# Cluster attention and expert layers on one core: a third of the exponential units take an fp16 upper part written by ScalarE, and leave out the product of the two low parts

## The chip, the core and the metric

The kernel runs on one core of one Trainium2 chip. The metric is device time in microseconds (us) of one launch. The engines are named as in the profile: PE (TensorE matmuls), PEld (its weight loads), DVE (VectorE), ACT (ScalarE), POOL (GpSimd) and SP (the DMA queue that most loads are issued on).

## The reference, cut to what matters

Attention over 4 batches, 8 heads, 768 positions, 64 numbers a head, with a mask that lets a query see only keys of its own cluster. Its output goes through a two-level mixture of 16 experts, one expert a row.

```
q_assign = argmax(q_n . c_n); k_assign = argmax(k_n . c_n)
mask   = q_assign[:, :, :, None] == k_assign[:, :, None, :]
scores = where(mask, q @ k.T / sqrt(64), -1e9)
attn   = exp(scores - max(scores)); attn /= sum(attn) + 1e-9
out    = attn @ v
x      = out as 3072 rows of 512
y      = combined gate * (relu(x @ w1[e]) @ w2[e])      # e: the row's expert
```

## The kernel before, in words

**Two stages.** The attention stage takes 32 (batch, head) pairs one after the other; the text calls them heads 0 to 31. Then an expert stage streams the 16 experts' weights from HBM. Everything in fp32 is carried as an upper part and a low part in 16 bits each, so that matmuls run on 16-bit operands.

**A head is 9 units.** The 768 x 768 scores of a head are cut into 9 units of 128 keys x 512 queries. For each unit u of head h the program records `fine(h, u)`, one or two units of `coarse` of a later head, `av` of the unit five before (`LAG = 5`), and then what is due `beside`: loads, splitting of q, k and v into parts, cluster assignment, masks, router logits.

- `fine`: PE makes the scores of the unit into a PSUM tile `psf` (two buffers; L346 and L347). ACT takes the exponential into an SBUF tile `p32` in fp32 (L351; the profile calls it `p`). The upper part `ph` is no tile of its own: it is every second 16-bit word of `p32`, read as bf16. POOL (for five units of each of the last two heads DVE) subtracts it from `p32` and writes the low part `pl` in fp16 (L353).
- `coarse`: PE makes scores of a later head into `psc` (two buffers; L304) and DVE takes row maxima of them (L307).
- `av`: for each of the unit's four blocks of 128 queries, four matmuls of 64 or 65 columns add to the head's output `pso`: `ph` and `pl`, each against the upper part of v (`vh`, 65 columns, one of them of ones for the denominator) and against its low part (`vl`, 64 columns). Each has a weight load of its own.

**What sets the order.** The program text gives each instruction a priority; a scheduler then places the instructions on the engines, each engine in order. So an instruction more on one engine can move others, on that engine and on the rest. `p32`, `pl` come from a pool of seven buffers each.

Of the kernel before, what the change touches and what calls it, by code (L numbers as in the profile page):

```python
# [11 lines left out]
F16 = mybir.dt.float16  # L12
BF16 = mybir.dt.bfloat16
# [9 lines left out]
P = 128  # L23
# [9 lines left out]
def attention(ctx, tc, qT, kT, vr, cen, R, DEN, cfg):  # L33
    nc = tc.nc
# [4 lines left out]
    NCH = S // P  # L39
# [10 lines left out]
    EARLY = ()  # L50
    GAP, RM, RL = 1, 2, 8
    DVE_LO = [()] * 8
    DVE_END = (0, 2, 4, 6, 8)

    const = ctx.enter_context(tc.tile_pool(name="aconst", bufs=1))
# [3 lines left out]
    pp = ctx.enter_context(tc.tile_pool(name="pp", bufs=LAG + 2))  # L59
# [275 lines left out]
    def fsegs(u):  # L335

        return [(r % NCH, r // NCH * (S // 2) + x0, r // NCH * (S // 2) + x1) for r, x0, x1 in segs(u, S // 2)]

    def fine(h, u):
        assert ("max", h) in ready  # L340
        pf = ps_f.tile([P, 512], F32, name="psf")
        off = 0
        for (c, q0, q1) in fsegs(u):
            o = pf[:, off:off + q1 - q0]
            ks = slice(c * P, (c + 1) * P)
            nc.tensor.matmul(out=o, lhsT=KA[h % 8][0:82, ks], rhs=QA[h % 8][0:82, q0:q1], start=True, stop=False)  # L346
            nc.tensor.matmul(out=o, lhsT=KBs[h][:, ks], rhs=QBs[h][:, q0:q1], start=False, stop=True)  # L347
            off += q1 - q0
        p32 = pp.tile([P, 512], F32, name="p32")
        pl = pp.tile([P, 512], F16, name="pl")  # L350
        cfg["exp"] = nc.scalar.activation(out=p32, in_=pf, func=AF.Exp, scale=QK / (SQ * SQ))  # L351
        ph = p32.bitcast(BF16)[:, 1::2]
        lo = (nc.vector if u in (EARLY if h < 2 else DVE_LO[h % 8] if h < NH - 2 else DVE_END) else nc.gpsimd).tensor_tensor(out=pl, in0=p32, in1=ph, op=ALU.subtract)  # L353
        if lo.ins.engine == ET.Pool:
            cfg["lo"] = lo
        Ph[h, u], Pl[h, u] = ph, pl

    def av(h, u):

        vt = V[(h // 2) % 4]  # L360
        off = 0
        ph, pl = Ph.pop((h, u)), Pl.pop((h, u))
        if u == 0:
            Os[h] = ps_o.tile([P, 512], F32, name="pso")
        O = Os[h]
        for (c, q0, q1) in fsegs(u):
            vh, vl = vt[:, h % 2, c, 64:129], vt[:, h % 2, c, 0:64]
            for q in range(q0 // P, q1 // P):
                bs = slice(off, off + P)
                col = q * OW  # L370
                for i, p in enumerate((ph, pl)):
                    nc.tensor.matmul(out=O[:, col:col + 65], lhsT=p[:, bs], rhs=vh, start=c == 0 and q == 0 and i == 0, stop=False, skip_group_check=True)  # L372
                    nc.tensor.matmul(out=O[:, col:col + 64], lhsT=p[:, bs], rhs=vl, start=False, stop=c == NCH - 1 and i == 1, skip_group_check=True)  # L373
                off += P
        if u == 8:
            finish(h)

    def finish(h):

        O = Os.pop(h)  # L380
        b, hh = h // H, h % H
        if hh == 0:
            XSt[b] = xsp.tile([P, NCH, 2, H * D], F16, name="xs")
        Ov = O[:, 0:NCH * OW].rearrange("p (c w) -> p c w", w=OW)
        den = DEN[:, h]
        nc.vector.tensor_scalar(out=den, in0=Ov[:, :, 64], scalar1=EPS, scalar2=1.0 / XS, op0=ALU.add, op1=ALU.mult)
        rec = sm.tile([P, NCH], F32, name="rec")
        nc.vector.reciprocal(out=rec, in_=den)
        xs = XSt[b][:, :, :, hh * D:(hh + 1) * D]
        x = Ov[:, :, 0:64]  # L390
        nc.vector.tensor_tensor(out=x, in0=x, in1=rec.broadcast_to([P, NCH, D]), op=ALU.mult)
        nc.scalar.copy(out=xs[:, :, 0], in_=x)
        nc.vector.tensor_tensor(out=xs[:, :, 1], in0=x, in1=xs[:, :, 0], op=ALU.subtract)
# [94 lines left out]
    def av_next(g):  # L488
        h, u = prev.pop(0)
        av(h, u)  # L490
        if u == 8:
            b, hh = h // H, h % H
            last = b == B - 1 and hh == H - 1
            if last:
                cfg["xs"] = XSt[b]
            if hh == H - 1:
                R.store(b, XSt[b])
            if hh % 2 == 1:
                gens = [R.logits(b, XSt[b], hh // 2, [(ps_m, "psm"), (ps_f, "psf")] if last else None)]
                if hh == H - 1 and not last:  # L500
                    XSt.pop(b)
                    gens += [R.decide(b, then=(lambda: go(now[0], cfg["first"]())) if b == B - 2 else None)]
                at(g + RL, go, g + RL, itertools.chain(*gens))
# [5 lines left out]
    for h in range(NH):  # L509
        for u in range(9):  # L510
            fine(h, u)
            while n < min(9 * NH, g + 1 + min(AHEAD, AHEAD0 + g // 4)):
                coarse(n // 9, n % 9)
                if n % 9 == 8:
                    at(g + 1, go, g + 1, rowmax(n // 9))
                n += 1
            prev.append((h, u))
            if len(prev) > LAG:
                av_next(g)
            beside(g)  # L520
            g += 1
# [846 lines left out]
def tile_cluster_attention_moe(ctx, tc, qT, kT, vr, cen, wr, w1, w2, out):  # L1368
# [25 lines left out]
    with ExitStack() as c:  # L1394
        attention(c, tc, qT, kT, vr, cen, R, DEN, cfg)
# [53 lines left out]
```

## Time and profile before

| | |
|---|---|
| time, median of 3 runs | 765.72 us (764.88 to 766.91) |
| the profiled execution: its own time | 770.1 us |
| its span, first to last instruction | 768.3 us |
| mean granted TensorE clock | 0.984 |
| busy over the span: PE / PEld / DVE / ACT / POOL | 95% / 82% / 79% / 61% / 65% |
| attention stage, first to last L346 matmul | 24.9 to 418 us |

The profiled execution is 1.8 us longer than its span, and 4.4 us longer than the median of the runs. Busy shares are means over both stages; "idle before" in the rows below is the time that an engine stood still just before the instructions of a group, with what ended most of it. A busy PE is not PE at its peak, because matmuls are pipelined: one record lasts some 190 ns while the next begins 30 ns later.

### The profile page before, as it was taken

Reading aid. Unit: us, or ns where it says so; the run is one execution under the profiler, and the core shown is the slowest. Engines: PE = TensorE matmul, PEld = TensorE weight load, DVE = VectorE, ACT = ScalarE, POOL = GpSimd, SP = SyncE. Lnnn points to the kernel's source line nnn. Section 1 sums busy time; section 2 is a strip of 40 time slices with the busy share of each in tenths; the row PEclk is TensorE's granted clock in tenths of the full one; section 3 lists DMA queues with packets and bytes.
Section 4 is the critical chain, followed back from the end, with each engine's and each line's share of the span. In section 5 each row is a group of like instructions: output and inputs, shape, how many; then the busy total and the mean of one; then the engine's idle time right before and its main releaser. Section 6 shows DMA issues by size and latency. Waiting matters only on the chain. (4 is left out here: it accounts for less than half of the span.)

```text
span 768.3 us, 26718 instructions
## 1 busy us (share of the span) xinstructions
PE 731.0 (95%) x11086; PEld 626.9 (82%) x11086; DVE 605.7 (79%) x1209; ACT 466.6 (61%) x910; POOL 499.6 (65%) x522
## 2 busy tenths in 40 slices
PE   5899999999999999998999989999999999999996
PEld 3667888878888788886778777788779999999996
DVE  5887978899788997988866645867588898889861
ACT  4556876868778687674977346435534455555542
POOL 9577778779887798876884425526555556655532
PEclk9889999999999999999999999999999999999999
DMA  8857424545345461231420489866777788888821
GB/s 247 198 144 182 127 74 125 157 112 142 72 129 171 92 147 52 65 126 61 112 80 3 99 270 311 262 212 211 242 236 237 239 272 262 263 277 277 260 81 49
DMA packets 80392, 128.28 MB, mean 167 GB/s; under 512 B 8851, under 2 KB 47251, under 8 KB 80264
## 3 DMA queue, kind: packets, MB, share of 16 engines
q1 hardware_dynamic: 74492, 113.12, 50.7%
q0 software_dynamic: 5616, 13.35, 5.0%
q8 instruction: 88, 1.44, 0.9%
q14 instruction: 40, 0.33, 0.2%
q10 hardware_dynamic: 156, 0.03, 0.0%
HBM read 93.20 MB, written 14.11 MB: 140 GB/s over the span
## 5 line engine op out<-in xcount | busy, mean ns | idle before, releaser
L353 POOL TENSOR_TENSOR pl<-p 128x512 f16<-128x512 f32 x278 | 286.3, 1048 | 86.0 <-ACT p L351 81.1
L307 DVE TENSOR_REDUCE mpart<-psc 128x1 f32<-128x512 f32 (+1 forms) x282 | 190.2, 683 | 34.9 <-PE psc L304 34.8
L351 ACT ACTIVATE p<-psf 128x512 f32<-128x512 f32 x288 | 168.8, 595 | 58.2 <-PE psf L347 54.1
L372 PE MATMUL pso<-V,p 128*128 128x65 f16 x1152 | 162.6, 194 | 0.0
L372 PE MATMUL pso<-V,pl 128*128 128x65 f16 x1152 | 162.1, 194 | 0.0
L373 PE MATMUL pso<-V,pl 128*128 128x64 f16 x1152 | 161.9, 192 | 0.0
L373 PE MATMUL pso<-V,p 128*128 128x64 f16 x1152 | 161.8, 192 | 0.0
L346 PE MATMUL psf<-A 82*128 82x384 f16 (+2 forms) x576 | 145.7, 278 | 4.8 <-ACT p L351 3.2
L347 PE MATMUL psf<-B 128*128 128x384 f16 (+2 forms) x576 | 146.3, 278 | 0.0
L373 PEld LDWEIGHTS <-p 128*128 128x128 bf16 x1152 | 113.1, 98 | 21.7 <-issue 0.7
L372 PEld LDWEIGHTS <-p 128*128 128x128 bf16 x1152 | 112.6, 98 | 8.8 <-issue 0.8
L373 PEld LDWEIGHTS <-pl 128*128 128x128 f16 x1152 | 113.2, 98 | 0.4
L304 PE MATMUL psc<-A 80*128 80x512 f16 (+1 forms) x376 | 109.6, 332 | 4.1 <-DVE mpart L307 2.9
L372 PEld LDWEIGHTS <-pl 128*128 128x128 f16 x1152 | 111.7, 97 | 0.3
L959 DVE SCALAR_TENSOR_TENSOR hl<-psh,hh 128x160 f16<-128x160 f32 (+14 forms) x136 | 50.1, 371 | 60.3 <-ACT hh L958 60.1
L958 ACT ACTIVATE hh<-psh 128x160 f16<-128x160 f32 (+14 forms) x136 | 46.5, 347 | 69.0 <-PE psh L956 68.6
L956 PE MATMUL psh<-xT,wh0a 128*128 128x288 f16 (+7 forms) x512 | 74.7, 255 | 0.0
L347 PEld LDWEIGHTS <-B 128*128 128x128 f16 x576 | 57.4, 100 | 14.7 <-issue 6.4
L956 PE MATMUL psh<-xT,wh0b 128*128 128x272 f16 (+6 forms) x448 | 65.2, 254 | 0.9 <-ACT xT L930 0.9
L346 PEld LDWEIGHTS <-A 82*128 82x128 f16 x576 | 56.3, 99 | 11.0 <-issue 1.1
L918 POOL DMA_INDIRECT xg<-xbuf,ri x32 | 40.8, 1274 | 36.2 <-issue 17.8
L956 PE MATMUL psh<-xT,wl0a 128*128 128x288 f16 (+7 forms) x256 | 64.0, 255 | 0.0
(311 smaller groups left out, 1752.5 us busy)
## 6 DMA issues: line engine op xcount, KB each, us to landing
st<-w SPq DMA_DIRECT2D x128, 512.0 KB
B<-parts SPq DMA_DIRECT2D x64, 192.0 KB
kx<-kT SPq DMA_DIRECT2D x16, 384.0 KB
qx<-qT SPq DMA_DIRECT2D x16, 384.0 KB
vx<-vr SPq DMA_DIRECT2D x16, 384.0 KB
A<-parts SPq DMA_DIRECT2D x32, 192.0 KB
xbuf<-xs SPq DMA_DIRECT2D x4, 1536.0 KB
A<-mk SPq DMA_DIRECT2D x56, 24.0 KB
```

What stands on the lines that cost most here:

```text
L304: last["mm"] = nc.tensor.matmul(out=pc[:, off:off + k1 - k0], lhsT=QA[h % 8][0:80, c * P:(c + 1) * P], rhs=KA[h % 8][0:80, k0:k1], start=T ...
L307: nc.vector.tensor_reduce(out=(mp[:, 0, 0:1], mp[:, :, 1], mp[:, 1, 0:1])[i], in_=pc.rearrange("p (a x) -> p a x", a=n), axis=AX.X, op=ALU ...
L346: nc.tensor.matmul(out=o, lhsT=KA[h % 8][0:82, ks], rhs=QA[h % 8][0:82, q0:q1], start=True, stop=False)
L347: nc.tensor.matmul(out=o, lhsT=KBs[h][:, ks], rhs=QBs[h][:, q0:q1], start=False, stop=True)
L351: cfg["exp"] = nc.scalar.activation(out=p32, in_=pf, func=AF.Exp, scale=QK / (SQ * SQ))
L353: lo = (nc.vector if u in (EARLY if h < 2 else DVE_LO[h % 8] if h < NH - 2 else DVE_END) else nc.gpsimd).tensor_tensor(out=pl, in0=p32, in ...
L372: nc.tensor.matmul(out=O[:, col:col + 65], lhsT=p[:, bs], rhs=vh, start=c == 0 and q == 0 and i == 0, stop=False, skip_group_check=True)
L373: nc.tensor.matmul(out=O[:, col:col + 64], lhsT=p[:, bs], rhs=vl, start=False, stop=c == NCH - 1 and i == 1, skip_group_check=True)
L918: self.got = nc.gpsimd.indirect_dma_start(out=xg[0:n].rearrange("p a d -> p (a d)"), out_offset=None, in_offset=bass.IndirectOffsetOnAxis( ...
L956: self.mm = nc.tensor.matmul(out=ph[:, 0:M], lhsT=w[:, k, fs], rhs=xT[:, a, k], start=i == 0, stop=i == 3 * KD - 1)
L958: nc.scalar.activation(out=hh[:, f], in_=ph[:, 0:M], func=AF.Relu)
L959: self.ev = nc.vector.scalar_tensor_tensor(out=hl[:, f], in0=ph[:, 0:M], scalar=0.0, in1=hh[:, f], op0=ALU.max, op1=ALU.subtract)
```

## The change

For units 1, 4 and 7 of every head (`WHOLE16`) ACT writes the upper part as an fp16 tile `ph` of its own, with a copy from `p32` that rounds; POOL (or DVE) subtracts that tile. In `av` of these units the fourth product, `pl` against `vl`, is not made: three matmuls for each block of queries instead of four. The other six units of a head stay as they are. The new tile has three buffers.

```diff
+    WHOLE16 = 1, 4, 7
...
         cfg["exp"] = nc.scalar.activation(out=p32, in_=pf, func=AF.Exp, scale=QK / (SQ * SQ))
-        ph = p32.bitcast(BF16)[:, 1::2]
+        if u in WHOLE16:
+            ph = pp.tile([P, 512], F16, name="ph", bufs=len(WHOLE16))
+            nc.scalar.copy(out=ph, in_=p32)
+        else:
+            ph = p32.bitcast(BF16)[:, 1::2]
         lo = (nc.vector if u in (EARLY if h < 2 else DVE_LO[h % 8] if h < NH - 2 else DVE_END) else nc.gpsimd).tensor_tensor(out=pl, in0=p32, in1=ph, op=ALU.subtract)
...
-                for i, p in enumerate((ph, pl)):
-                    nc.tensor.matmul(out=O[:, col:col + 65], lhsT=p[:, bs], rhs=vh, start=c == 0 and q == 0 and i == 0, stop=False, skip_group_check=True)
-                    nc.tensor.matmul(out=O[:, col:col + 64], lhsT=p[:, bs], rhs=vl, start=False, stop=c == NCH - 1 and i == 1, skip_group_check=True)
+                prods = [(ph, vh), (ph, vl), (pl, vh)] + ([] if u in WHOLE16 else [(pl, vl)])
+                for i, (p, v) in enumerate(prods):
+                    nc.tensor.matmul(out=O[:, col:col + v.shape[-1]], lhsT=p[:, bs], rhs=v, start=c == 0 and q == 0 and i == 0, stop=c == NCH - 1 and i == len(prods) - 1, skip_group_check=True)
```

Five lines more stand above these places, so L351 becomes L352, L353 becomes L358 and L372/L373 become L378; the new copy is L355.

The order on PE, in `av` of unit 1 of head 0, the first unit that the change touches. Before, a block of 128 queries is eight rows (`p_566` is the unit's `p32`):

```order
L372 LDWEIGHTS p_566
L372 MATMUL pso<-V_173,p_566 128x65
L373 LDWEIGHTS p_566
L373 MATMUL pso<-V_173,p_566 128x64
L372 LDWEIGHTS pl
L372 MATMUL pso<-V_173,pl 128x65
L373 LDWEIGHTS pl
L373 MATMUL pso<-V_173,pl 128x64
```

In the changed kernel a block of the same unit is six rows:

```order
L378 LDWEIGHTS ph
L378 MATMUL pso<-V_173,ph 128x65
L378 LDWEIGHTS ph
L378 MATMUL pso<-V_173,ph 128x64
L378 LDWEIGHTS pl
L378 MATMUL pso<-V_173,pl 128x65
```

The last weight load and the last matmul of 64 columns are gone, here and in 383 other blocks; PE has 384 loads and 384 matmuls less.

The order on ACT, from the exponential of unit 4 of head 8 to the one of unit 7 and what follows it. Before (L351 is the exponential, L200 a half of a split, L222 and L180 splits of v, q and k, L392 the upper part of a head's output, L599 a copy for the router):

```order
L351 ACTIVATE p_3309<-psf 128x512
L222 ACTIVATE V_176<-vx 128x12x64
L351 ACTIVATE p_3357<-psf 128x512
L200 ACTIVATE psm<-vx 128x384
L351 ACTIVATE p_3389<-psf 128x512
L392 CAST xs<-pso 128x6x64
L351 ACTIVATE p_3421<-psf 128x512
L180 ACTIVATE parts<-qx 128x768
L180 ACTIVATE parts<-kx 128x768
```

The changed kernel at the same place, from the exponential of unit 4 on (L355 is the new copy, L201 the half split, L223 and L181 the splits):

```order
L352 ACTIVATE p_3263<-psf 128x512
L201 ACTIVATE psm<-vx 128x384
L355 CAST ph<-p_3263 128x512
L352 ACTIVATE p_3313<-psf 128x512
L223 ACTIVATE V_176<-vx 128x12x64
L352 ACTIVATE p_3345<-psf 128x512
L397 CAST xs<-pso 128x6x64
L352 ACTIVATE p_3373<-psf 128x512
L201 ACTIVATE psm<-vx 128x384
L355 CAST ph<-p_3373 128x512
L352 ACTIVATE p_3407<-psf 128x512
L181 ACTIVATE parts<-qx 128x768
```

Two copies have come in, each with a half split between its exponential and itself; the split of v and the two splits of q and k stand an exponential later than before. Over the whole kernel ACT has 96 copies more; 53 stand right behind their exponential, 43 have another instruction between.

## Rows read from the trace of the kernel before

**Rows 1.** The page: busy time of each engine over the whole span, and the granted TensorE clock in 40 slices, in tenths of full speed.

```profile
PE 731.0 (95%) x11086; PEld 626.9 (82%) x11086; DVE 605.7 (79%) x1209; ACT 466.6 (61%) x910; POOL 499.6 (65%) x522
...
PEclk9889999999999999999999999999999999999999
```

**Rows 2.** Busy time of each engine in the attention stage, 24.9 to 418.2 us: stretch, its length, then busy us (and instructions) of PE, PEld, DVE, ACT and POOL, the granted clock, the DMA share and GB/s.

```profile
24.90:418.20 393.30, 377.38 (x7135) 313.58 (x7134) 336.85 (x733) 292.01 (x561) 306.27 (x298) 0.98 0.42 113
```

**Rows 3.** What PE waited for from 20 to 423 us: us in total, times, the longest.

```profile
PE psm L655 <- DVE roe L643: 4.1, 3, 1.4
PE psf L346 <- ACT p L351: 3.2, 5, 1.6
PE psc L304 <- DVE mpart L307: 2.9, 6, 0.8
```

**Rows 4.** The timeline of PE in head 14: start, us of the record, line. The rows left out are 14 more `av` matmuls of the same unit.

```profile
212.94 0.19 PE L372 MATMUL pso<-V,p 128*128 128x65 f16 x1
...
213.39 0.19 PE L373 MATMUL pso<-V,pl 128*128 128x64 f16 x1
213.42 0.33 PE L346 MATMUL psf<-A 82*128 82x384 f16 x1
```

**Rows 5.** Groups of instructions of the whole kernel: line, engine, operation, shapes, how many | busy us, mean ns of one | idle time before them. The weight loads of both parts, and the subtraction on POOL.

```profile
L353 POOL TENSOR_TENSOR pl<-p 128x512 f16<-128x512 f32 x278 | 286.3, 1048 | 86.0 <-ACT p L351 81.1
...
L373 PEld LDWEIGHTS <-p 128*128 128x128 bf16 x1152 | 113.1, 98 | 21.7 <-issue 0.7
...
L373 PEld LDWEIGHTS <-pl 128*128 128x128 f16 x1152 | 113.2, 98 | 0.4
```

**Rows 6.** Groups of ACT from 20 to 423 us, each shape apart, in the same columns: the exponential, a split that reads SBUF and writes 768 columns of fp16, and a scaling that reads 512 columns of SBUF.

```profile
L351 ACT ACTIVATE p<-psf 128x512 f32<-128x512 f32 x288 | 168.8, 595 | 58.2 <-PE psf L347 54.1 <-POOL pl L353 2.9 <-PE psc L304 0.5
...
L180 ACT ACTIVATE parts<-qx 128x768 f16<-128x768 f32 x14 | 11.8, 840 | 3.7 <-PE psm L241 2.8 <-DMA vx<-vr 0.8
...
L787 ACT ACTIVATE psm<-st 128x512 f32<-128x512 f32 x16 | 9.7, 605 | 0.0
```

**Rows 7.** A timeline of DVE and ACT in head 14: an ACT instruction that waits for a DVE result.

```profile
203.20 0.17 DVE L313 TENSOR_REDUCE m<-mpart 128x6 f32<-128x18 f32 x1
...
203.41 0.21 ACT L317 ACTIVATE mh<-m 128x6 f16<-128x6 f32 x1 [0.25 <-DVE m L313]
```

**Rows 8.** The timeline of ACT where head 8 ends and head 9 begins (at 140.2 us): start, us, line, in brackets the idle time before.

```profile
139.49 0.84 ACT L180 ACTIVATE parts<-qx 128x768 f16<-128x768 f32 x1 [0.32 <-DMA vx<-vr]
140.24 0.83 ACT L180 ACTIVATE parts<-kx 128x768 f16<-128x768 f32 x1
140.97 0.58 ACT L351 ACTIVATE p<-psf 128x512 f32<-128x512 f32 x1
141.45 0.49 ACT L200 ACTIVATE psm<-vx 128x384 f32<-128x384 f32 x1
141.86 0.59 ACT L351 ACTIVATE p<-psf 128x512 f32<-128x512 f32 x1
142.34 0.80 ACT L599 COPY xTr<-psm 128x768 f16<-128x768 f16 x1
143.11 0.99 ACT L266 ACTIVATE mk<-psm,mbias,mscale 128x768 f16<-128x768 f16 x1
144.00 0.20 ACT L317 ACTIVATE mh<-m 128x6 f16<-128x6 f32 x1
144.10 1.24 ACT L351 ACTIVATE p<-psf 128x512 f32<-128x512 f32 x2
```

**Rows 9.** Busy time of the engines head by head, in the columns of rows 2. A stretch begins with the first L346 matmul of its head, to a tenth of a us. First heads 11 to 18, then heads 28 to 31.

```profile
166.20:177.90 11.70, 11.51 (x236) 9.62 (x233) 10.67 (x22) 8.14 (x17) 10.90 (x11) 1.00 0.49 121
177.90:189.50 11.60, 11.50 (x234) 9.56 (x231) 11.56 (x27) 9.89 (x21) 11.12 (x12) 1.00 0.67 189
189.50:202.80 13.30, 13.26 (x258) 11.25 (x255) 10.05 (x23) 10.88 (x20) 11.50 (x13) 1.00 0.29 62
202.80:213.40 10.60, 10.60 (x207) 8.83 (x204) 9.17 (x20) 8.25 (x18) 9.57 (x10) 1.00 0.44 119
213.40:224.70 11.30, 11.30 (x234) 9.53 (x231) 9.07 (x18) 7.49 (x16) 9.37 (x10) 1.00 0.27 70
224.70:236.40 11.70, 11.60 (x237) 9.67 (x234) 11.66 (x27) 10.08 (x21) 9.47 (x10) 1.00 0.69 188
236.40:249.40 13.00, 12.97 (x255) 11.10 (x252) 9.67 (x22) 10.27 (x19) 9.33 (x10) 1.00 0.49 167
249.40:262.00 12.60, 11.24 (x219) 9.25 (x216) 12.39 (x35) 8.02 (x18) 8.45 (x9) 1.00 0.23 67
...
372.50:383.50 11.00, 11.00 (x215) 9.23 (x212) 9.47 (x21) 9.62 (x19) 10.63 (x11) 1.00 0.33 58
383.50:397.40 13.90, 12.10 (x221) 10.08 (x218) 9.34 (x24) 10.29 (x20) 13.32 (x14) 0.95 0.35 92
397.40:409.00 11.60, 10.80 (x215) 9.20 (x213) 8.49 (x18) 10.51 (x21) 6.23 (x8) 0.91 0.08 24
409.00:418.20 9.20, 9.20 (x187) 8.26 (x187) 6.46 (x15) 8.08 (x15) 4.15 (x4) 1.00 0.02 4
```

**Rows 10.** Who waited from 20 to 423 us, in the columns of rows 3: ACT for the scores.

```profile
ACT p L351 <- PE psf L347: 54.1, 94, 2.3
```

**Rows 11.** A group of POOL from 20 to 423 us: the one other subtraction of an fp16 tile from an fp32 one.

```profile
L187 POOL TENSOR_TENSOR V<-vx,V 128x768 f16<-128x768 f32 x1 | 1.6, 1587 | 0.0
```

## The prediction

> **What bounds the kernel now.** I read the page's busy shares first. Over the whole span PE is busy 95%, ACT 61% [rows 1]; the change touches the attention stage alone, so I took that stage by itself: of 393.30 us PE is busy 377.38, DVE 336.85, POOL 306.27, ACT 292.01 [rows 2]. Then the list of what PE waits for. It is short: 4.1 us for a DVE result of the router, 3.2 us for exponentials, 2.9 us for row maxima [rows 3]. Then whether a busy PE there is a full one, since its records overlap: in the timeline the sixteen `av` matmuls of a unit begin from 212.94 to 213.39, 0.45 us for 15 steps, and the scores of the next unit begin 0.03 us after the last [rows 4]. PE has no gap there. In heads 14 and 15 it is busy 10.60 of 10.60 and 11.30 of 11.30 us [rows 9]. So PE sets the pace of this stage, and a matmul that is not made is time saved, as long as no other engine takes over.
>
> That other engine is looked for head by head, because a mean over the stage hides it. DVE is full in heads 12 and 16 (11.56 of 11.60, 11.66 of 11.70) and nearly in head 18 (12.39 of 12.60); ACT has its most in heads 12, 13, 16 and 17 (9.89 of 11.60, 10.88 of 13.30, 10.08 of 11.70, 10.27 of 13.00) and again in 28, 30 and 31 [rows 9]. Yet ACT mostly waits for PE: exponentials waited 54.1 us for scores [rows 10].
>
> **What the rule on occupancy would make of it.** In head 15, where PE is busy 11.30 of 11.30 us, the weight loads are busy 9.53 us, 84%; over the stage 313.58 of 393.30, 80% [rows 2, 9]. The Trainium skill (Perfetto Trace Analysis, Identifying the Most-Contended Engine) says that matmul occupancy is a bad measure of how near TensorE is to its limit, and that the share of weight loads should be read instead. By that rule PE would have a fifth of the stage spare and the saving would come out of slack, for no change at all; by the timeline PE has no gap at 84%. Here the steps of 30 ns decide, and the rule goes into a rival below.
>
> **What the change removes.** 3 units x 32 heads x 4 blocks = 384 matmuls of 64 columns with their loads. One step is 0.45 / 15 = 0.030 us [rows 4]: 384 x 0.030 = **11.5 us**, or 0.36 us a head. The remaining loads read contiguous fp16 in place of every second 16-bit word; loads of the strided `p` and of the contiguous `pl` take 98 ns each [rows 5], so the step should stay.
>
> **What it adds on ACT.** 96 copies, 128x512 from fp32 to fp16. The trace has none of this form. From above: a split of 768 columns takes 840 ns; from below and near it: a scaling of 512 columns from SBUF takes 605 ns, an exponential of 512 columns 595 ns [rows 6]. I take 0.60. What a copy costs ACT depends on its place. Independent ACT instructions overlap by 0.10 us (the exponential at 140.97 lasts 0.58 and the next begins at 141.45 [rows 8]). A copy right behind its exponential can't overlap it: it waits for its end and some 0.04 us for the signal (a DVE result at 203.20 + 0.17 is taken up by ACT at 203.41 [rows 7]; this case has no ACT instruction that waits for the one before it). So 53 copies put 0.64 us between the exponential and what follows, and 43 with another instruction between put 0.50: 33.9 + 21.5 = 55.4 us, 0.58 a copy, 1.73 us a head. At nothing it can't be costed everywhere, and in full it can't cost either: 393.30 - 292.01 = 101 us of ACT are free [rows 2], but not where they are needed.
>
> **Where ACT falls short.** For each head of rows 9 I set the length less 0.36 (what PE would now need) against ACT's busy time plus 1.73. Short are head 12 (11.24 against 11.62: 0.38), head 16 (11.34 against 11.81: 0.47), head 28 (10.64 against 11.35: 0.71), head 30 (11.24 against 12.24: 1.00) and head 31 (8.84 against 9.81: 0.97). Heads 13, 14 and 17 have only 0.33, 0.26 and 0.64 to spare; heads 11, 15, 18 over 1.4. The same pattern of splits, masks and router work comes every 8 heads, so I count rows 11 to 18 three times for heads 3 to 26: 3 x 0.85 + 2.68 = 5.2 us. That is the lower end of what ACT takes back, for it lets ACT work at 100% of a head.
>
> The upper end goes by the one head in which PE waited for exponentials and ACT was the fuller engine: head 30, ACT 10.51 of 11.60 us, 0.906 [rows 9]. If ACT can never be filled beyond that, a head lasts (ACT + 1.73) / 0.906 where this is more: 1.59 over in head 12, 0.98 in 13, 0.78 in 14, 1.70 in 16, 0.61 in 17, 1.89 in 28, 2.27 in 30, 1.99 in 31. 3 x 5.66 + 6.15 = 23.1 us.
>
> I take a value nearer the lower end: 5.2, and 0.35 more in each of the nine heads like 13, 14 and 17, 3.2 us, together **8.4 us**. Two rows speak for the lower end. ACT ran without a gap from 139.49 to 145.34 [rows 8] and in head 13, the same place of the pattern, PE is busy 13.26 of 13.30 us [rows 9]: the two `psf` buffers carry PE over a late exponential of about a unit. And ACT's busy time counts a lone instruction in full, where in a queue 0.10 of it overlaps. What speaks for more is that two copies enter just this stretch, 1.1 us of delay against buffers that hold about one unit.
>
> **What is late next, and the rest.** The delayed exponential is waited for by PE (the scores after next want its `psf`), and through it by DVE. In heads 10, 18 and 26 DVE leaves 0.21 us of the 0.36 (12.39 of 12.60 [rows 9]): 3 x 0.15 = 0.45 us lost. In 12 and 16 DVE leaves 0.04, but there ACT's shortage has taken the saving already, so it isn't counted twice. The subtraction now waits for the copy, up to 0.64 us later; behind it on POOL stand the subtractions of the next units, and `av` five units on waits for them. POOL stood idle 86.0 us before its subtractions, nearly all of it for exponentials [rows 5], and PE's list holds no wait for `pl` [rows 3], so this costs nothing; without that cover it would be up to 96 x 0.64 = 61 us. The subtraction itself reads fp16 in place of strided bf16: 1.048 us for 512 columns [rows 5] against 1.587 for 768 with a contiguous fp16 operand [rows 11], which is 1.058 for 512: no change. `ph` has three buffers for three units a head and is read five units on, so nobody waits for a buffer. The expert stage starts when attention ends and moves with it.
>
> **The sum.** 770.1 - 11.5 + 8.4 + 0.45 = 767.5 us for an execution like the profiled one (its span 768.3 and 1.8 around it), 2.6 less than it. That one lies 4.4 above the median, 765.72, so **763.1 us** is what I predict.
>
> **The rivals.**
> - *ACT takes over.* As the upper end: no filling of ACT beyond 0.906, 23.1 us lost for 11.5 saved, +12 us at the end of it, 778; halfway, +5.5, 771. For it speaks that seven of the twelve heads of rows 9 would have ACT over 0.95 full (12, 13, 14, 16, 28, 30, 31). Against it the stretch of rows 8. It decides against the change once ACT's price passes 11.5 - 0.45 = 11.05 us, 0.12 a copy.
> - *The copies hide.* The scheduler puts splits later and copies behind other work, as the ACT order shows twice, and ACT's shortage in a head is made up in the next. Then 11.5 less 0.5 to 2, 754.7 to 756.2. Against it heads 28 to 31, which have no easy head behind them.
> - *Nothing comes of it.* PE is not the bound, or the saving is used up by ACT and by DVE's full heads in equal parts: 765.7, from 763.5 to 768. The trace's short list of waits speaks against the first half. By the Trainium skill's rule on weight loads (Perfetto Trace Analysis, Identifying the Most-Contended Engine) this would be the likely case.
>
> **How the numbers follow.** About 0.3%, 2.3 us, is what a measurement can tell here from no change. The forecast, a small gain of 0.5 to 6 us (759.7 to 765.2): 0.50, of which 0.33 beyond 2.3 us and 0.17 within. The hidden copies 0.13, nothing 0.12, ACT taking over 0.25. Faster 0.33 + 0.13 = 0.46, the same 0.17 + 0.12 = 0.29, slower 0.25. The range reaches to all but the ends of both: 756 (half of the hidden copies' cases lie lower) to 772 (two fifths of ACT's cases lie higher), some 0.17 left out.
>
> **What would show it.** In the trace of the changed kernel PE's `av` matmuls fall by 384 and step 30 ns still; the copies take 0.60; ACT's busy time in the stage rises by 50 to 57 us, to some 345 of 390; PE's waits for exponentials rise from 3 to about 10 us, most in heads like 12, 13, 28, 30 and 31; heads 15 and 18 get shorter by 0.2 to 0.36 us, head 30 longer. Wrong it would be if copies cost over 0.7 us each with their wait (then slower), if the scheduler fills PE's waits with `av` (then faster), or if PE waits for `pl`.

## The result, and the profile after

| | kernel before | changed kernel |
|---|---|---|
| median | 765.3 us (764.72 to 766.91, 4 runs) | 773.31 us (772.24 to 773.82, 4 runs) |
| ratio, 95% interval | | 1.0099 [1.008, 1.0119] |
| the profiled execution: time, span, clock | 770.1, 768.3, 0.984 | 772.24, 770.4, 0.977 |

The changed kernel is 8.0 us slower. The prediction was a gain of 2.6 us, 763.1 us, in a range of 756 to 772; sign and range were wrong.

The profiled execution of before is 4.8 us above this median, that of the changed kernel 1.1 below its own. So the kernel before was profiled a second time (768.0 us, span 766.3, clock 0.992), and the comparisons are with that execution unless the first is named. A head is measured from its first score matmul on PE to that of the next head; head 3 starts at 67.8 us in the second profile of before (its row below begins 0.1 us later) and at 67.0 in the changed kernel.

The page of the changed kernel, busy time and clock, in the place of [rows 1]:

```profile
PE 723.3 (94%) x10702; PEld 615.9 (80%) x10702; DVE 611.3 (79%) x1209; ACT 509.9 (66%) x1006; POOL 502.3 (65%) x522
...
PEclk7899999999999999999999999999999999999998
```

Its groups of the exponential's subtraction on POOL, without and with the new tile, and of the copy [rows 5, 6]:

```profile
L358 POOL TENSOR_TENSOR pl<-p 128x512 f16<-128x512 f32 x184 | 189.5, 1046 | 26.2 <-ACT p L352 13.9
...
L358 POOL TENSOR_TENSOR pl<-p,ph 128x512 f16<-128x512 f32 x94 | 110.0, 1170 | 52.2 <-issue 26.6
...
L355 ACT CAST ph<-p 128x512 f16<-128x512 f32 x96 | 59.3, 617 | 1.7
```

Stretches of the kernel before, second profile, in the columns of rows 2: from head 3 to the end of the attention stage, then head 10.

```profile
67.90:419.00 351.10, 338.80 (x6632) 285.00 (x6633) 300.51 (x663) 263.86 (x513) 279.68 (x274) 1.00 0.38 104
151.40:164.00 12.60, 11.24 (x219) 9.25 (x216) 12.39 (x35) 8.05 (x18) 8.42 (x9) 1.00 0.27 83
```

The changed kernel: the same stretch, head 10, a part of head 10, heads 12, 14 and 26, and where head 29 ends.

```profile
67.00:423.70 356.70, 336.62 (x6276) 277.26 (x6276) 302.89 (x662) 304.12 (x602) 288.21 (x274) 0.99 0.38 103
150.10:165.60 15.50, 12.42 (x209) 10.00 (x206) 14.69 (x37) 10.23 (x22) 9.12 (x10) 0.89 0.15 41
158.80:162.00 3.20, 3.20 (x34) 2.40 (x33) 3.02 (x14) 2.23 (x5) 1.07 (x1) 0.50 0.22 55
176.50:187.90 11.40, 11.07 (x222) 9.00 (x219) 11.05 (x26) 10.19 (x23) 11.21 (x11) 1.00 0.73 181
201.80:212.10 10.30, 10.30 (x196) 8.53 (x193) 8.90 (x20) 9.48 (x21) 9.75 (x10) 1.00 0.42 118
343.80:359.30 15.50, 12.42 (x209) 9.86 (x206) 15.23 (x42) 8.70 (x18) 9.30 (x10) 0.89 0.01 2
397.50:401.00 3.50, 3.50 (x40) 2.53 (x38) 3.41 (x9) 3.27 (x5) 3.47 (x4) 0.51 0.25 75
```

Two things are to be seen. Head 14 is 0.37 us shorter than before, within a hundredth of what was predicted for a head that PE fills. And head 10 is 2.8 us longer, with fewer matmuls: PE does less in it, at a mean clock of 0.89, because for 3.4 us the granted clock is 0.50, its lower level of 1.2 GHz. From head 3 to the end of the attention stage there are three such stretches of 3.4 us, in heads 10 and 26 and at the end of head 29. PE is busy throughout, so each adds some 1.7 us of busy time, half of itself (an estimate). The second profile of before has none in this part.

**The account from head 3 on.** The stretch grew by 5.6 us (351.1 to 356.7). PE's busy time fell by 2.2; without the 5.1 us that the half clock adds it fell by 7.3. The time in which PE stood grew from 12.3 to 20.1, by 7.8. So 5.6 = -7.3 + 5.1 + 7.8. By 0.36 us a head the 29 heads from 3 on should have given 10.4; the other 3.1 us are not placed. What PE waited for, changed kernel, 20 to 430 us, in the columns of rows 3 and in answer to them:

```profile
PE psm L660 <- DVE roe L648: 7.1, 3, 3.1
PE psm L601 <- DVE idA L847: 4.2, 1, 4.2
PE psc L305 <- DVE mpart L308: 3.1, 5, 0.9
PE psm L264 <- ACT xTr L604: 2.4, 5, 0.5
PE psf L347 <- ACT p L352: 2.2, 9, 0.4
PE psm L329 <- ACT mh L318: 1.9, 7, 0.3
```

The wait for `roe`, the longest of [rows 3] already, grew from 4.1 to 7.1 us; waits for the router table (`idA`) and for `xTr` are new. The wait for exponentials, where the prediction looked for the loss, fell to 2.2, from 3.2 in the first profile of before and 4.7 in the second.

Lengths of heads in us, from the timelines of PE (before is its second profile; the kernels of the last five columns are described below):

| head | before | changed | product only | copies only | subtraction on DVE | off the router | router only |
|---|---|---|---|---|---|---|---|
| 10 | 12.62 | 15.45 | 14.71 | 14.66 | 11.80 | 12.62 | 14.33 |
| 12 | 11.63 | 11.40 | 11.18 | 12.02 | 15.71 | 11.45 | 11.63 |
| 13 | 13.03 | 13.84 | 13.12 | 13.79 | 13.23 | 13.85 | 14.00 |
| 14 | 10.65 | 10.28 | 10.29 | 10.64 | 10.28 | 10.28 | 10.64 |
| 15 | 11.33 | 10.97 | 10.98 | 11.32 | 10.97 | 10.97 | 11.33 |
| 18 | 12.62 | 13.07 | 12.66 | 15.68 | 11.74 | 12.63 | 16.75 |
| 26 | 13.43 | 15.45 | 13.71 | 15.67 | 13.18 | 13.36 | 16.57 |
| 27 | 13.90 | 12.94 | 18.16 | 13.26 | 17.02 | 14.06 | 12.85 |
| 29 | 12.70 | 16.21 | 13.82 | 13.12 | 16.35 | 14.04 | 13.35 |

### The profile page after: what moved, and what is told of

It is laid out like the page before. It is cut to its first block, busy times and chain, and to the rows that moved or that the text cites. A ratio compares the mean times of both kernels' runs of the same rounds, so it can differ in the third digit from the quotient of the medians.

```text
span 770.4 us, 26026 instructions
## 1 busy us (share of the span) xinstructions
PE 723.3 (94%) x10702; PEld 615.9 (80%) x10702; DVE 611.3 (79%) x1209; ACT 509.9 (66%) x1006; POOL 502.3 (65%) x522
## 3 DMA queue, kind: packets, MB, share of 16 engines
q0 software_dynamic: 5616, 13.35, 4.9%
## 5 line engine op out<-in xcount | busy, mean ns | idle before, releaser
L358 POOL TENSOR_TENSOR pl<-p 128x512 f16<-128x512 f32 x184 | 189.5, 1046 | 26.2 <-ACT p L352 13.9
L352 ACT ACTIVATE p<-psf 128x512 f32<-128x512 f32 x288 | 170.5, 598 | 33.9 <-PE psf L348 32.1
L378 PE MATMUL pso<-V,pl 128*128 128x65 f16 (+1 forms) x1920 | 160.6, 194 | 0.1
L358 POOL TENSOR_TENSOR pl<-p,ph 128x512 f16<-128x512 f32 x94 | 110.0, 1170 | 52.2 <-issue 26.6
L378 PEld LDWEIGHTS <-pl 128*128 128x128 f16 x1920 | 131.1, 98 | 1.9 <-DVE pl L358 0.2
L378 PEld LDWEIGHTS <-p 128*128 128x128 bf16 x1536 | 109.0, 98 | 21.8 <-issue 3.6
L378 PE MATMUL pso<-V,p 128*128 128x65 f16 (+1 forms) x1536 | 117.2, 193 | 0.0
L355 ACT CAST ph<-p 128x512 f16<-128x512 f32 x96 | 59.3, 617 | 1.7
L1037 POOL DMA_INDIRECT out_dram<-y,ri x32 | 39.3, 1227 | 32.1 <-ACT y L1036 26.2
L961 PE MATMUL psh<-xT,wl0b 128*128 128x272 f16 (+6 forms) x224 | 55.9, 253 | 0.0
```

What stands on the lines that cost most here:

```text
L355: nc.scalar.copy(out=ph, in_=p32)
L378: nc.tensor.matmul(out=O[:, col:col + v.shape[-1]], lhsT=p[:, bs], rhs=v, start=c == 0 and q == 0 and i == 0, stop=c == NCH - 1 and i == l ...
L961: self.mm = nc.tensor.matmul(out=ph[:, 0:M], lhsT=w[:, k, fs], rhs=xT[:, a, k], start=i == 0, stop=i == 3 * KD - 1)
```

## What happens in head 10

The timeline of PE in head 10 of the changed kernel: start, us of the record, instruction. The first rows are `av` of a unit with three products; then comes the router's first rank matmul, L660, which L655 was.

```profile
154.40 0.22 PE L378 MATMUL pso<-V,ph 128*128 128x65 f16 x2
154.46 0.19 PE L378 MATMUL pso<-V,pl 128*128 128x65 f16 x1
154.49 0.22 PE L378 MATMUL pso<-V,ph 128*128 128x65 f16 x2
...
154.73 0.20 PE L378 MATMUL pso<-V,pl 128*128 128x65 f16 x1
158.00 0.20 PE L660 MATMUL psm<-roe,low 128*128 128x96 f16 x1 [3.08 <-DVE roe L648]
```

A block of three matmuls takes 0.09 us: the step is 30 ns, as predicted. A step after the row at 154.73 PE has come to L660, and it stands until 158.00, and everything behind it in PE's order stands with it. What it wants, `roe`, is the end of a chain on DVE that begins when the logits are there. The two-input instructions of that chain, and below them POOL at the same time:

```profile
152.22 0.98 DVE L635 TENSOR_TENSOR req<-lg,rmx 128x120 f16<-128x120 f32 x1
153.72 0.90 DVE L636 TENSOR_TENSOR req<-req,desc 128x120 f16<-128x120 f16 x1
154.55 1.14 DVE L643 TENSOR_TENSOR rdf<-lg,rmx 128x120 f32<-128x120 f32 x1
155.91 0.28 DVE L640 TENSOR_TENSOR roh<-req,rmw 128x120 f16<-128x120 f16 x1
156.89 1.06 DVE L648 TENSOR_TENSOR roe<-roh 128x96 f16<-128x96 f16 x1
```

```profile
151.03 2.04 POOL L358 TENSOR_TENSOR pl<-p 128x512 f16<-128x512 f32 x2 [0.37 <-ACT p L352]
153.39 1.15 POOL L358 TENSOR_TENSOR pl<-p,ph 128x512 f16<-128x512 f32 x1 [0.33 <-POOL pl L358]
154.51 1.04 POOL L358 TENSOR_TENSOR pl<-p 128x512 f16<-128x512 f32 x1
156.80 1.04 POOL L358 TENSOR_TENSOR pl<-p 128x512 f16<-128x512 f32 x1 [1.25 <-ACT p L352]
```

Four of the five take 0.90 to 1.14 us, and each of these begins while a subtraction runs on POOL and ends 0.08 to 0.14 us after it (`rdf` at 155.69, POOL at 155.55). The fifth, `roh`, begins in a gap of POOL and takes 0.28. In the first profile of the kernel before the same five were:

```profile
155.74 0.85 DVE L630 TENSOR_TENSOR req<-lg,rmx 128x120 f16<-128x120 f32 x1
...
157.12 0.45 DVE L631 TENSOR_TENSOR req<-req,desc 128x120 f16<-128x120 f16 x1
157.50 0.27 DVE L638 TENSOR_TENSOR rdf<-lg,rmx 128x120 f32<-128x120 f32 x1
...
157.99 0.82 DVE L635 TENSOR_TENSOR roh<-req,rmw 128x120 f16<-128x120 f16 x1
...
159.51 0.46 DVE L643 TENSOR_TENSOR roe<-roh 128x96 f16<-128x96 f16 x1
```

Together 2.85 us there and 4.36 in the changed kernel: 1.5 us more, which is most of what PE's longest wait grew by (1.4 in [rows 3], 3.1 here). The instructions are the same; the moments at which POOL's subtractions start against them are not. Head 18 of the changed kernel bears this out: there the five take 0.59, 0.21, 0.27, 0.94 and 0.30 us, 2.31 together, and PE's wait for `roe` is 0.9 us, less than before. The Trainium skill (SBUF — State Buffer, SBUF: two separate sides) says that VectorE instructions with two SBUF inputs and GpSimd instructions that read SBUF share a pair of ports, which one of them holds for its whole instruction while the other is blocked. The rows agree, with a stand of up to 0.87 us (1.14 against 0.27).

So head 10: 1.7 us more of standing, 1.7 us by estimate for 3.4 us at half clock behind it, 0.36 us less of matmuls: +3.0, measured +2.8. The estimate for the clock is a high one: head 10 of the kernel "router only" has the same wait of 3.1 us at a clock of 1.00 and lasts 14.33 us, 1.1 less than here.

## The experiments

Two theories at the start. A: ACT, by its copies, takes back the saving. B: PE in order stands at a DVE result, chiefly the rank matmul, and a faster PE only gets there earlier. The ratio is always to the kernel before, run on the same chip.

**The kernel before again**, no edit: 1.0005 [0.9979, 1.0031].

> The kernel before, profiled once more. Its profiled execution shown ahead of the prediction took 770.1 us, 4.4 over the median of its runs; the changed kernel's profiled execution took 772.2, 1.1 under its median. Both theories expect a time of 765 to 767 us. If the first profile was an unlucky execution, this one has a span of some 763 to 766 us, and its first three heads (45.1 us in the first profile, 41.4 in the changed kernel's) take some 41 us; if profiling costs this kernel 4 us, the span is again some 768.

Its span of 766.3 us and its first three heads, 42.6 us, lie between the two cases.

**The product alone, no copies.** It leaves `pl` times `vl` out of the output in these units.

```diff
-        if u in WHOLE16:
-            ph = pp.tile([P, 512], F16, name="ph", bufs=len(WHOLE16))
-            nc.scalar.copy(out=ph, in_=p32)
-        else:
-            ph = p32.bitcast(BF16)[:, 1::2]
+        ph = p32.bitcast(BF16)[:, 1::2]
```

> The product of the two low parts is left out in units 1, 4 and 7, but the upper part stays every second 16-bit word of p32 and no copy is made (so the part of the output that comes from low part times low part of these units is missing). Theory A (ACT's 96 copies take back what PE saves): 11.5 us faster than before at most, 754 to 758 us, and the router's rank matmuls wait no longer than before (4.1 us in three waits). Theory B (a new order puts the router's matmuls ahead of their inputs, whatever ACT does): 760 us or more, with 7 us of waits at the rank matmuls. Rival that PE is not the bound: 765 us, no change.

763.14 us, 0.9983 [0.9949, 1.0017]: with no copy at all, 1.3 us by the ratio are left of the saving of 11.5 (between 3.9 and a loss of 1.3 by the interval; the medians lie 2.8 apart). Its waits, 20 to 425 us, and its head 10:

```profile
PE psm L656 <- DVE roe L644: 6.3, 3, 2.5
PE psm L597 <- DVE wl L789: 3.6, 1, 3.6
```

```profile
148.00:162.70 14.70, 12.24 (x208) 9.89 (x205) 14.24 (x36) 8.65 (x19) 9.00 (x9) 0.88 0.20 54
```

Heads 14 to 16 give 0.36 to 0.45 us each; heads 10, 26, 27 and 29 take back 7.8 in this profile. This is B in its wide sense: PE stands at a late DVE result. The rank matmul is the smaller part of it, since head 27, where PE waits for `wl`, is 4.3 us longer, and heads 10, 18 and 26 together 2.4.

**The copies alone**, all four products made:

```diff
-                prods = [(ph, vh), (ph, vl), (pl, vh)] + ([] if u in WHOLE16 else [(pl, vl)])
+                prods = [(ph, vh), (ph, vl), (pl, vh)] + [(pl, vl)]
```

> The copies are made and their fp16 tile is used, but all four products stay. Theory A: the changed kernel plus the 11.5 us of matmuls that are back, or less where ACT now sets the pace: 779 to 785 us. If ACT fully set the pace, the matmuls would be free and it would take the changed kernel's 773. Theory B: 773 to 780, with the waits of 7 us at the rank matmuls as in the changed kernel.

780.19 us, 1.0209 [1.0163, 1.0255]: 16 us by the ratio, in A's range and just above B's. Its waits, 20 to 430 us:

```profile
PE psm L660 <- DVE roe L648: 8.9, 3, 3.0
PE psm L264 <- ACT xTr L604: 4.1, 5, 1.2
```

Heads 14 and 15 hide their copies whole, heads 12 and 16 pay 0.4, heads like 13 0.5 to 0.8, and heads 10, 18 and 26 pay 2.0 to 3.1, since the wait for `roe` grew here too, without a faster PE. So the copies alone are enough for it; whether by the order that they make or by ACT's time, this run doesn't separate. What heads like 13 pay is mostly a wait for ACT (`xTr`, 0.61 us in heads 13, 17 and 21), and that part is A's.

**The change in half of the heads**, 14 with room for ACT:

```diff
-        if u in WHOLE16:
+        if u in WHOLE16 and h % 4 in (2, 3) and h < 28:
```

(and so in `av`).

> The change in heads 2, 3, 6, 7, 10, 11 and so on to 27 alone (14 of 32), where ACT had most time to spare (1.4 us a head and more in all but heads like 14). Theory A: 14 x 0.36 = 5.0 us saved, about 1 given back: 760 to 763 us, the waits for the mask's matmuls in heads like 13 (0.63 us) gone. Theory B: the waits at the rank matmuls stand in heads 10, 18 and 26, which have copies here, so they stay at 7 us and the time is 765 to 768.

772.65 us, 1.0108 [1.0076, 1.0139]: 42 of the 96 copies, where ACT is free, and the whole loss; heads 10 and 18 are 2.9 and 3.9 us longer. Both ranges were missed, A's by more: A alone is out, and B was priced too low.

**The rank matmuls later.** If PE stands at the first rank matmul, recording them two units later should let the chain finish. In the changed kernel, in the one before, and with the product alone left out:

```diff
-        yield PSM, 1, 1
+        yield PSM, 3, 1
```

> The changed kernel with the router's rank matmuls (L660, three times in the stage) issued two units later. Theory B (PE, in order, stands behind a rank matmul whose input the VectorE chain has not finished, 7.6 us in three waits): these waits fall below 1 us, heads 10, 18 and 26 go from 15.45, 13.07, 15.45 us to some 12 each, and the time to 764 to 767 us. Theory A (ACT's load costs the time, the place of the wait is only where it shows): the lost time turns up elsewhere and the kernel stays at 771 to 774.

> The kernel before with the same later place of the rank matmuls. Theory B: it had 4.6 us of these waits, 1.52 in each of heads 10, 18 and 26, so it falls by 3 to 4.5 us to 761 to 763. Theory A: no change, 765 to 766.

> The product alone left out (as before in this study: the part of the output from low part times low part of units 1, 4 and 7 is missing, no copies), with the later rank matmuls. Theory B: heads 10, 18 and 26 lose their waits of 6.8 us, and the whole saving of the matmuls is seen against the kernel before with the same place: 11 us less, 750 to 753. If the saving is lost whatever the place: 760 or more.

A miss for B: 779.12, 775.82 and 775.03 us beside 770.29 for before on this chip: 1.0119 [1.0061, 1.0178], 1.0063 [1.0038, 1.0089], 1.007 [1.004, 1.01]. The changed kernel is about where it was without the edit, as A says; that the kernel before got slower neither theory expected. The wait for `roe` is gone from all three, and others came; the changed kernel with the edit, 20 to 430 us:

```profile
PE psc L305 <- DVE mpart L308: 11.4, 19, 1.5
PE psm L329 <- DVE wl L793: 4.0, 1, 4.0
```

and the kernel before with it:

```profile
PE psf L346 <- ACT p L351: 4.1, 3, 2.4
PE psm L328 <- DVE wl L788: 2.6, 1, 2.6
```

DVE is the fuller engine in the router heads (in the changed kernel 14.69 of 15.50 us in head 10 and 15.23 of 15.50 in head 26, before 12.39 of 12.60), so PE may only stand for its row maxima in place of its ranks. In the kernel before the edit made heads 10, 18 and 26 shorter by 0.7 to 1.6 us, to 11.9 each, as B says, and heads 11 and 19 longer by 0.8. What it lost there stands in heads 27 and 30, 3.1 and 3.2 us longer, with the two waits shown and three stretches of 3.4 us at half clock. So the place of the rank matmul doesn't settle the time; that DVE's time in the router heads is the price is a reading, not shown.

**The router heads' subtractions on DVE**, so that POOL runs none beside the chain:

```diff
-    DVE_LO = [()] * 8
+    DVE_LO = [()] * 2 + [(0, 1, 2, 3)] + [()] * 5
```

> The changed kernel with the subtractions of units 0 to 3 of heads 2, 10, 18 and 26 on VectorE in place of GpSimd. Claim to be tested: VectorE's router operations that read two SBUF tensors stretch because GpSimd's subtraction (1.05 us) runs at the same time. If so, rdf (1.14 us in heads 10 and 26), the product with desc (0.90) and roe (1.06) fall to their durations without GpSimd, 0.27, 0.21 and 0.26 us as after the stage's end. If not, they stay near 1 us. The time itself may go either way, since VectorE takes 4 x 0.71 us more in each of the heads: 767 to 774 us.

The chain in head 10:

```profile
155.28 0.27 DVE L635 TENSOR_TENSOR req<-lg,rmx 128x120 f16<-128x120 f32 x1
...
156.08 0.21 DVE L636 TENSOR_TENSOR req<-req,desc 128x120 f16<-128x120 f16 x1
...
157.00 0.27 DVE L643 TENSOR_TENSOR rdf<-lg,rmx 128x120 f32<-128x120 f32 x1
157.19 0.27 DVE L640 TENSOR_TENSOR roh<-req,rmw 128x120 f16<-128x120 f16 x1
...
158.34 0.25 DVE L648 TENSOR_TENSOR roe<-roh 128x96 f16<-128x96 f16 x1
```

This shows the cause of the long instructions: with POOL away all five fall to 0.21 to 0.27 us, and heads 10 and 18 to 11.80 and 11.74, below before; the wait for `roe` is 1.3 us in all. As a version it is none: 778.92 us, 1.0107 [1.0045, 1.0169]. Heads 12, 27 and 29 take it back (15.71, 17.02, 16.35): POOL beside the chain is a cause of head 10's length, not of the whole loss.

**The change off the router**: heads 1 and 2 of each eight and those from 25 on as before.

```diff
-    WHOLE16 = 1, 4, 7
+    WHOLE16, ROUTER = (1, 4, 7), (1, 2)
...
-        if u in WHOLE16:
+        if u in WHOLE16 and h % 8 not in ROUTER and h < 25:
```

> The change in heads 0, 3 to 8, 11 to 16 and 19 to 24 alone; heads 1, 2, 9, 10, 17, 18 and 25 to 31 as before. Theory B (the loss arises where the router's chain and the first expert's loads run, heads 10, 18, 26, 27 and 29, because queues in order line up differently there): summing the head lengths of the changed kernel and of the kernel before over these heads gives 3.5 to 4.5 us saved, so a ratio to the kernel before of 0.994 to 0.996, and heads 10 and 18 return to 12.6 us. Theory A (the 57 copies left still load ScalarE): 1.000 or above.

765.69 us, 1.0011 [0.9983, 1.0039]: the loss is gone, the gain that I expected did not come. Waits, 20 to 425 us:

```profile
PE psm L660 <- DVE roe L648: 4.0, 3, 1.4
...
PE psm L264 <- ACT xTr L604: 2.4, 5, 0.5
```

The ranks are back at [rows 3], heads 10 and 18 at 12.62 and 12.63, and no stretch from head 3 to the end of the stage is at half clock. The 19 heads gave 4.1 us of busy time, and PE stood 3.7 longer: the heads 5, 9, 13, 17 and 21, with mask work, are together 2.8 us longer, 9 and 17 of them without a copy of their own.

**Its complement**, the change in the other 13 heads alone (`u in WHOLE16 and (h % 8 in ROUTER or h >= 25)`):

> The complement of the first of these runs: the change in heads 1, 2, 9, 10, 17, 18 and 25 to 31 alone, 13 of 32. Theory B: the loss is made here, as in the run with heads 2, 3 modulo 4: heads 10, 18, 26 or 29 are longer by 2 to 3 us each, ratio 1.008 to 1.016. Theory A: 39 copies of 96 cost two fifths of what all cost: 1.003 to 1.005.

775.42 us, 1.0123 [1.008, 1.0165], as expected: the whole loss sits with the 13 heads; 10, 18 and 26 are 1.7, 4.1 and 3.1 us longer.

**The product alone off the router**, and in all nine units of those heads (`WHOLE16 = range(9)`), both without copies; both leave that product out of the output:

> The product alone left out in the same 19 heads (the part of the output from low part times low part of units 1, 4 and 7 of these heads is missing, no copies). Theory B: the head lengths of the run with the product alone give 7.4 us saved, 19 x 0.36 = 6.8 by the matmuls: ratio 0.990 to 0.992. If the saving of a matmul is lost wherever it is made: 0.997 to 1.000.

> The same with the product left out in all nine units of the 19 heads (low part times low part of these heads is missing altogether). 19 x 36 matmuls of 0.030 us are 20.5 us. Theory B with VectorE as the next bound (11.6 us of work in heads like 12 and 16, 12.4 in 18): heads like 14 and 15 fall by 1.0 each, heads like 12 by 0.1 at most; 12 to 16 us in all, ratio 0.979 to 0.985.

761.98 us, 0.9944 [0.9922, 0.9966], and 759.87 us, 0.9914 [0.9882, 0.9946]. By 30 ns a step 228 and 684 matmuls are 6.8 and 20.5 us; 4.3 and 6.6 came, both less than B expected. The saving is real off the router and has an end: three times the matmuls gave half as much again. Beside the kernel with copies in the same heads, 1.0011, the copies cost 0.0067 of 766, some 5 us, or 0.09 a copy.

**Fewer heads.** Heads like 5 and 13 left out as well (`ROUTER = (1, 2, 5)`); then the change only in heads 6 and 7 of each eight up to 23 (`h % 8 in ROOMY`), and in 3, 6 and 7:

> The change in heads 0, 3, 4, 6, 7, 8, 11, 12, 14, 15, 16, 19, 20, 22, 23 and 24 alone: as in the run off the router, less heads 5, 13 and 21. If the copies within heads 5, 13 and 21 make the mask's matmuls wait for ScalarE (0.64 us a head there), these heads return to 13.0 to 13.6 us, the saving of the others stays (0.24 in heads like 12, 0.36 in heads like 14 and 15), and the ratio to the kernel before is 0.994 to 0.998. If the copies at the end of the head in front (unit 7 of heads 4, 8, 12, 16, 20) do it, heads 5, 9, 13, 17 and 21 stay at 13.85 and the ratio is 0.999 to 1.002.

> The change in the two roomy heads of the pattern alone (heads 6, 7, 14, 15, 22, 23); the other 26 heads as before. If copies do harm only through the heads with mask work, router work or a full VectorE, and through the heads just ahead of these, the six heads keep their 0.36 us each: 2.2 us, ratio 0.996 to 0.998, no wait for roe over 1.5 us and no stretch at half clock behind one. If copies cost something everywhere, ratio 0.999 to 1.003.

> As the run with heads 6, 7, 14, 15, 22, 23, and head 3 of each eight as well (3, 11, 19). Head 11 with its copies was 11.56 against 11.67 us where the heads around the router were left as before. If that 0.1 us is real: 2.2 + 0.3 = 2.5 us, ratio 0.995 to 0.998. If the copies of head 11 push the splits of head 12 later, heads 12 and 20 get longer by 0.2 or more and it is no better than the other run.

No gain in any: 1.0048 [1.0027, 1.0069], above both of its ranges, 1.0002 [0.9973, 1.0031] and 1.0003 [0.9978, 1.0028], without the gain hoped for. In the first, heads 5, 13 and 21 stay at 13.84 us without copies, as its second case says, and head 29 lasts 16.02. In the second, heads 7, 15 and 23 keep 0.36 us and heads 6, 14 and 22 0.13, and heads 13 and 17, without a copy in them or in the head ahead, are at 13.98 and 13.90 against 13.03 and 13.02, behind a wait for another tile (`V` L202, not `xTr`). So two things lengthen the mask heads. The wait for `xTr` stands in the profile of every kernel with copies in heads 4, 8, 12, 16 and 20, the ones just ahead of the mask heads, and in none without. And a changed order elsewhere is enough for the wait for `V`; which instruction's place does that is open.

**The changed kernel once more**, for a second profile:

> The changed kernel once more, for a second profile. Ratio 1.008 to 1.012. If TensorE's clock falls because it stands for some 3 us behind the first rank matmul, the waits for roe in heads 10 and 26 are 3.1 us again and the granted clock is 0.5 for some 3.4 us behind at least one of them, so that such a head lasts 14.3 us without and 15.5 to 16.8 with it. If the fall was an accident of that execution, the waits are there and the clock stays at 1.0 behind both.

1.0103 [1.0054, 1.0152]. The wait for `roe`, 20 to 430 us; then head 10, a part of it, and head 26:

```profile
PE psm L660 <- DVE roe L648: 7.1, 3, 3.1
```

```profile
150.00:165.40 15.40, 12.32 (x207) 9.89 (x204) 14.67 (x37) 10.15 (x22) 9.03 (x10) 0.89 0.14 41
159.20:162.40 3.20, 3.20 (x36) 2.25 (x34) 2.99 (x11) 2.70 (x6) 1.57 (x2) 0.50 0.37 119
344.60:360.00 15.40, 12.32 (x207) 9.89 (x204) 15.16 (x40) 8.62 (x18) 9.28 (x10) 0.89 0.01 2
```

The same heads, the same wait, the same fall of the clock: it is no accident of one execution. Nor is it a certain price: with the copies alone head 10 has the wait (3.0 us) at a clock of 1.00 and lasts 14.66 us, and in the complement 14.33 at 1.00, while its heads 18 and 26 have two such stretches each and last 16.75 and 16.57. I didn't try to keep PE busy through the wait.

## Why the prediction was wrong, point by point

**The removal.** 384 matmuls at 30 ns: right, and seen where PE is the engine that sets the pace (heads 14, 15, 22 and 23 by 0.36 to 0.37 us each). That it showed in full in heads where weight loads are busy 83% of the time answers the prediction's third rival. The Trainium skill (Perfetto Trace Analysis, Identifying the Most-Contended Engine) would have the share of weight loads read for TensorE's room; here that share was no measure of it.

**The failed step is "What is late next, and the rest".** There heads 10, 18 and 26 were priced at 0.45 us, as what DVE's filling leaves of the saving, and heads 27 and 29 at nothing, without a reason. The product alone, without a copy, sizes that term: 11.5 us expected, 1.3 measured, so about 10 us went to it. In the profile of that kernel heads 10, 18 and 26 are 2.4 us longer in place of 1.1 shorter, and heads 27 and 29 5.4 longer in place of 0.7 shorter. From head 3 on, PE's busy time fell by 11.7 us without the half clock, the clock took 5.1 (by the estimate above) and standing 4.7. With the copies in place, more of the saving came: from the copies alone, 1.0209, to the whole change, 1.0099, are 8.4 us of the 11.5. So the term is 3 to 10 us by the order in which it is sized, and 0.45 in neither. Three things were missed. I took DVE's durations as fixed, though [rows 3] put a DVE chain on top of PE's waits and POOL runs beside it; they grew by 1.5 us in one head. I counted DVE's spare time as the limit, but PE waits in order for one result, so its wait grows by as much as the chain is late, not by what DVE lacks. And I gave a wait of PE no second price, though [rows 9] showed a clock of 0.95 and 0.91 in heads 29 and 30 of the kernel before: 13.9 x 0.05 + 11.6 x 0.09 = 1.7 us, the estimate for one such stretch.

**The copies.** 0.60 us was taken and 0.617 measured. ACT's busy time in the attention stage rose by 43.5 us, from 292.7 to 336.2, 0.45 a copy in place of the 0.58 of the prediction. What the copies take back, 8.4 us by the prediction, is 0.0116 of 766, about 9 us, between the product alone and the whole change, and 0.09 a copy off the router. That this is near 8.4 is luck: without the removal the same copies cost 16 us, and they did it another way. PE's waits for exponentials, predicted to rise to 10 us, fell to 2.2; heads 12 and 16 got 0.23 to 0.25 shorter, and head 18 longer where it was to be shorter. Head 30, which was to be longer, says nothing: 11.60 and 12.12 in the two profiles of before, 11.91 and 11.83 after. The cost lies in the mask heads, the router heads and head 29. So the rival "ACT takes over", nearest in time at 771 to 778, was not the mechanism as told: ACT has 9.48 of 10.30 us in head 14 (0.92) and 10.19 of 11.40 in head 12 without holding PE up there. But ACT has a share by another way: PE's waits for `p`, `mh` and `xTr` are 6.5 us in the changed kernel, against 2.3 with the product alone.

**POOL.** "No change" for the subtraction was off by 0.12 us: 1.170 us with the fp16 tile, 1.046 with the strided word. PE still hardly waited for `pl`.

**The base.** Taking off the 4.4 us by which the profiled execution lay above its median was right; its second profile is 2.1 us faster and lacks the half clock of heads 29 and 30.

**What stays open.** Head 29 waits for the router table's DMA through DVE. It lasted 12.70 and 13.9 us in two executions of before, 16.21 and 15.96 in two of the changed kernel, and 11.18 to 16.35 in the other kernels; how much of its 3.5 us the change makes is open. Of the 8.0 us the profiles show 4.2; the rest lies in how far the two profiled executions are from their medians, and is not placed. Nor is it shown why the copies cost 16 us without the removal and 9 with it. No version with the copies beat the kernel before.

## What to carry to other kernels

Before a saving on an engine that runs in order is summed, go down its list of waits and ask of each what it becomes when the engine arrives earlier and the other engines' work shifts against the chain it waits for: the top entry, a mere 4.1 us in 393, grew to 7.1 here, with half-clock stretches behind it. Price a wait of a few us on PE twice, for the standing and for a stretch at half clock behind it. And where a scheduler places the instructions, test the removal and the addition apart and don't add them up: their prices were -1.3 and +16 us, not -11.5 and +8.4, and together +8.

## What the runs showed of the hardware

DVE instructions with two SBUF inputs stand while a subtraction runs on POOL: 0.27 us becomes 1.14, 0.21 becomes 0.90, 0.25 becomes 1.06, ending about 0.1 us behind POOL's; with POOL away they take 0.21 to 0.27. And TensorE's clock fell to 0.50 for 3.4 us, once or twice, at the end of or behind most, not all, of the waits of 2.5 to 4.2 us of a PE that had hardly stopped before, and behind some shorter ones (1.8 us in head 29 of the first profile of before, 1.5 with the product alone and the later ranks); the 1.4 us of the rank wait in the kernel before left it at 1.00.
